# A second level of the seven-product scheme: one product of a DFT stage made jointly for two position pairs, with outputs gated from PSUM and added up in the output tensor

## The chip, the cores and the metric

The kernel runs on one core of a Trainium2 chip. The metric is device time of one execution in microseconds, as the median of several runs.

## The reference

The input is x, 2048 positions by 512 channels, all in fp32. Two branches of it are mixed by a gate per position:

```
a = x @ Re(Wh).T ;  b = x @ Im(Wh).T             # 512 x 512 DFT of the channels
y = Re(Ws) @ a - Im(Ws) @ b                      # 2048 x 2048 DFT of the positions, real part
v = (relu(x @ W_gate) * (x @ W_up)) @ W_down     # 512 -> 1792 -> 512
g = sigmoid((x * gate_w).sum(-1))
out = g * y + (1 - g) * v
```

## The kernel before

**Precision.** Each fp32 operand is split into a high part (a copy to fp32r on ScalarE, "hi") and a low part (raw minus high on VectorE, "lo"). A product is three matmuls: low x high, high x low, high x high (PARTS). A matmul has a stationary operand of 128x128 and a moving one of 128x512, and adds into one PSUM bank of 128x512.

**The seven products.** Every matrix product in the kernel is cut into 2 x 2 blocks on each side and made with seven block products instead of eight (the Strassen-Winograd form). The products are numbered 1 to 7. For each the left and right operand is a block or a sum of blocks (LEFT, RIGHT, and the sums in Left and Sequence), and the results are combined in PSUM: product 1 (X) is copied, negated, into Y's banks, products 6 and 7 add to Y, T gets a copy of Y, product 4 adds to T, product 3 adds to 5's banks M. PSUM's eight banks are four pairs: x, m, y, t.

**The stages, in order.** A warm-up of WARM matmuls of 256 columns; Direct and 13 Blocks (gate and up projections, 96 and 84 matmuls each); in between them four SpectralBlocks (channel DFT, 84 each), which write a and b to `ad` in DRAM; two Downs (the down projection, 294 each, for positions 0-1023 and 1024-2047); four Sequences (the position DFT, 336 each): for m = 0 (real) and m = 1 (imaginary) and each position pair p = 0, 1, in the order (m, p) = (0,0), (0,1), (1,1), (1,0). The last one is the subclass Last.

**A Round** is the common class of Down and Sequence. Its left operand is a Left object, which holds a high and a low part in 4-tile pieces for each product; its right operand comes in pieces jj = 0..3, for each of which a product makes 12 matmuls (two halves of 128 output channels, two tiles, three parts). The products go in the order ORDER_Z = 1, 5, 6, 3, 7, 2, 4. In a Sequence the four blocks of the DFT matrix for each jj are loaded once; the sums for products 5 and 6 are made on VectorE, those for 7 and 4 by accumulating DMAs from GpSimd's queue (`r<-r`), each so many matmuls ahead (SUM). Each product's right operand is then split by ScalarE and VectorE (HI and LO matmuls ahead).

**The outputs.** Down stores each block of v to `vd` and its negation to `zd`. Sequences of m = 0 accumulate their block of y into `zd` by DMA, which so becomes y - v. Sequences of m = 1 accumulate `zd` into their own block, load v, multiply by the gate row, add v, and store to `out`. Last does this for blocks "11" and "21" from PSUM, after loading z and v early. The gate rows (1 x 1024 positions broadcast to 128 partitions) come from `gd` in DRAM, which gate_store writes.

**The order of work.** Every operation is registered with a key: `pe(n, f)` puts matmuls at the plan's running count of matmuls, `op(key, f)` puts anything else at a given count. Plan.order then lists all instructions by a model of durations: matmuls in program order, VectorE and ScalarE by due time, at most 40 keys ahead of an operation's own key (AHEAD), SP's and GpSimd's DMAs not ahead of it. All buffers of SBUF but a few small ones are units of 4 KB per partition; there are 51 (UNITS), and an instruction that starts a new buffer waits in the list until a unit is free. Loads are issued by SP (`load`), stores and accumulations by GpSimd (`store`, `accumulate`), each queue in its listed order.

Tile names in the profile: `ch`, `cl` high and low part of a right operand, `lh`, `ll` of a left one, `r` and `hr` raw right operands, `l` and `lr` raw and summed left ones, `s` a copy of a PSUM result, `z`, `n`, `v` outputs, `gg` a gate row, `ps` PSUM. Every operation is recorded at line 125, the helper that issues it.

Of the kernel before, what the change touches and what calls it, by code (L numbers as in the profile page):

```python
# [277 lines left out]
def kernel(ctx: ExitStack, tc, xP, xG, wf, wgu, wd, cr, ci, wri, gw, out):  # L278
# [32 lines left out]
    vd, zd = (hbm(n, NT, P, KD, N) for n in ("vd", "zd"))  # L311
    wb = hbm("wb", 8, P, 4, 2, P)
    gd = hbm("gd", NT * KD, P)
    gwt = Buf(plan, "gwt", [D], kind="fixed", tile=small.tile([P, D], F32, name="gwt"))

    gs = Buf(plan, "gs", [32], kind="fixed", tile=small.tile([P, 32], F32, name="gs"))

    gx = Buf(plan, "gx", [32], kind="fixed", tile=small.tile([P, 32], F32, name="gx"))
# [267 lines left out]
    def gate(t, key):  # L586
        g = [buf("gx") for _ in range(2)]

        def read(i):
            load(g[i].all, xG[t, :, 2 * i:2 * i + 2])  # L590

        def add(i):
            x, n = g[i // 2][:, i % 2], KD * t + i
            E().vector.scalar_tensor_tensor(x, x, 1.0, gwt[:], op0=OP.mult, op1=OP.mult,
                                            accum_out=gs[:, n:n + 1])

        def sigmoid():
            ts = slice(KD * t, KD * (t + 1))
            E().scalar.activation(gs[:, ts], gs[:, ts], AF.Sigmoid)

        for i in range(2):
            op(key - 50, read, i)
        for i in range(KD):
            op(key + 10 * i, add, i)
        op(key + 50, sigmoid)

    def gate_store():
        E().vector.transpose(gx.all, gs.all)
        for i in range(0, P, 32):
            load(gd[:, i:i + 32], gx[i:i + NT * KD])  # L610

    def gate_row(p, key):

        b = buf("gg")

        def go():
            load(b.all, gd[2 * KD * p:2 * KD * (p + 1)].rearrange("(j i) p -> j (i p)", j=2).partition_broadcast(P))
        op(key, go)
        return b
# [79 lines left out]
    class Left:  # L699
# [21 lines left out]
        def split(self, m, n, key, step):  # L721
            hi, lo = self.t[m, n] = [buf(f"l{x}{m}", [4, HD], F32R) for x in "hl"]
            raw, s = self.side(m, n), slice(self.tiles[n])
            if m == 4:
                op(key, lambda: E().scalar.activation(hi[:, s], raw[:, s], AF.Copy, scale=-1.0))
                op(key + step, lambda: E().vector.scalar_tensor_tensor(
                    lo[:, s], raw[:, s], -1.0, f32(hi[:, s]), op0=OP.mult, op1=OP.subtract))
            else:
                op(key, lambda: E().scalar.copy(hi[:, s], raw[:, s]))
                op(key + step, lambda: E().vector.tensor_sub(lo[:, s], raw[:, s], f32(hi[:, s])))  # L730
# [12 lines left out]

    SUM = {5: 40, 6: 40, 7: 170, 4: 140}

    class Round:


        def __init__(self, left, counts):
# [3 lines left out]
            for x in ORDER_Z:  # L753
                for jj, n in enumerate(counts):
                    self.at[x, jj] = key
                    key += 6 * n
# [3 lines left out]
            for x in ORDER_Z:  # L760
                for jj, n in enumerate(counts):
                    pe(6 * n, self.product, x, jj)
                self.evac(x, plan.now)
# [20 lines left out]
        def evac(self, x, key):  # L784
# [6 lines left out]
            elif x == 3:  # L791
                op(key, lambda: e.vector.tensor_add(o["12"].all, M, s[6].all))
                self.done("12", key + 6)
            elif x == 7:
                op(key, lambda: e.scalar.copy(T, Y))
                op(key + 8, lambda: e.vector.tensor_add(o["22"].all, Y, s[5].all))
                self.done("22", key + 14)
            elif x == 2:
                self.middle(key)
            elif x == 4:  # L800
                self.end(key)

        def middle(self, key):
            op(key, lambda: E().scalar.copy(self.o["11"].all, PAIRS["x"].all))
            self.done("11", key + 6)

        def end(self, key):
            op(key, lambda: E().scalar.activation(self.o["21"].all, PAIRS["t"].all, AF.Copy, scale=-1.0))
            self.done("21", key + 6)


    class Down(Round):
        HI, LO = 44, 36

        def __init__(self, left, q):
            self.q = q
            super().__init__(left, (2, 2, 2, 1))

# [7 lines left out]
        def done(self, b, key):  # L826
            t, es = 2 * self.q + int(b[1]) - 1, slice(2 * int(b[0]) - 2, 2 * int(b[0]))
            o, n = self.o[b], buf("n" + b)
            op(key, lambda: store(vd[t, :, es], o.all))
            op(key + 2, lambda: E().scalar.activation(n.all, o.all, AF.Copy, scale=-1.0))  # L830
            op(key + 8, lambda: store(zd[t, :, es], n.all))


    class Sequence(Round):
        HI, LO = 31, 24

        def __init__(self, left, m, p):
            self.m, self.p = m, p
            if m:
                self.g = gate_row(p, plan.now + (20 if isinstance(self, Last) else 100))  # L840
            super().__init__(left, (2, 2, 2, 2))

        def rights(self):
            at = self.at
            for jj in range(4):
                r = {b: buf(f"r{b}") for b in BLOCKS}
                for b, key in (("11", at[1, jj]), ("12", at[5, jj]), ("22", at[6, jj] - 10), ("21", at[2, jj] - 36)):
                    op(key - 90, lambda r=r, b=b, jj=jj: load(
                        r[b].all, (cr, ci)[self.m][2 * self.p + int(b[1]) - 1, int(b[0]) - 1, jj]))
                for x, (o, i) in {5: ("11", "12"), 7: ("12", "22"), 6: ("11", "22"), 4: ("11", "21")}.items():  # L850
                    f = (lambda o, i: accumulate(o, i)) if x in (4, 7) else (lambda o, i: combine(o, o, i, 1))
                    op(at[x, jj] - SUM[x], lambda f=f, r=r, o=o, i=i: f(r[o].all, r[i].all))
                for x in ORDER_Z:
                    self.split(x, jj, r[{1: "11", 3: "22", 5: "11", 7: "12", 6: "11", 2: "21", 4: "11"}[x]])

        def place(self, b):
            return 2 * self.p + int(b[1]) - 1, slice(None), slice(2 * int(b[0]) - 2, 2 * int(b[0]))

        def gate(self, b):
            return self.g[:, int(b[1]) - 1].unsqueeze(1).to_broadcast([P, 2, N])  # L860

        def done(self, b, key):
            o = self.o[b]
            if self.m == 0:
                op(key, lambda: accumulate(zd[self.place(b)], o.all))
                return
            v = buf("v")
            op(key, lambda: accumulate(o.all, zd[self.place(b)]))
            op(key + 20, lambda: load(v.all, vd[self.place(b)]))
            op(key + 62, lambda: E().vector.tensor_mul(o.all, o.all, self.gate(b)))  # L870
            op(key + 64, lambda: E().vector.tensor_add(o.all, o.all, v.all))
            op(key + 70, lambda: load(out[self.place(b)], o.all))

    class Last(Sequence):


        def prepare(self):

            for b, k in (("11", self.base + 110), ("21", self.base + 160)):
                z, v = buf("z"), self.v[b]  # L880
                op(k - 50, lambda b=b, z=z: load(z.all, zd[self.place(b)]))
                op(k - 50, lambda b=b, v=v: load(v.all, vd[self.place(b)]))
                op(k, lambda b=b, z=z: E().vector.tensor_mul(z.all, z.all, self.gate(b)))
                op(k + 2, lambda v=v, z=z: combine(v.all, v.all, z.all, 1))

        def rights(self):
            super().rights()
            self.v = {b: buf("v") for b in ("11", "21")}
            self.prepare()

        def part(self, b, n, p, sign):
            E().vector.tensor_mul(self.o[b][:, n], p[n], self.g[:, 0])
            combine(self.v[b][:, n], self.v[b][:, n], self.o[b][:, n], sign)

        def middle(self, key):
            for n in range(2):
                op(key, self.part, "11", n, PAIRS["x"], 1)
            op(key + 8, lambda: load(out[self.place("11")], self.v["11"].all))

        def end(self, key):  # L900
            t, _, es = self.place("21")
            for n in range(2):
                op(key - 6 + 6 * n, self.part, "21", n, PAIRS["t"], -1)
                op(key - 6 + 6 * n, lambda n=n: load(out[t, :, es.start + n], self.v["21"][:, n]))
# [3 lines left out]
    WARM = 18  # L908
# [99 lines left out]
    for n in range(2):  # L1008
        for b, k in (("11", 40), ("21", 60), ("22", 70), ("12", 150)):
            op(key + k + n, la.load, b, n)  # L1010
        for m, k in ((1, 84), (5, 126), (7, 168), (6, 210), (3, 250), (2, 314), (4, 354)):
# [67 lines left out]
```

## Time and profile before

| | |
|---|---|
| median of 3 runs | 796.81 us (796.44 to 797.32) |
| the profiled execution | 796.05 us, span 794.3 us |
| TensorE busy | 787.9 us, 3474 matmuls |
| VectorE busy | 550.1 us, 610 instructions |
| ScalarE busy | 387.2 us, 419 instructions |
| GpSimd busy | 101.7 us, 146 instructions |
| HBM | 103.55 MB read, 54.53 MB written |

The span is that of one execution as the hardware profiler took it; the time of the same execution is a little longer. Engines: PE is TensorE's matmuls and PEld its weight loads, DVE VectorE, ACT ScalarE, POOL GpSimd, SP SyncE, and a q behind a name is that engine's DMA queue. Matmuls overlap one another, so that the shown duration of one is longer than the distance from one start to the next. In a line of the groups stand the operation, out<-in, the form, the count, the busy time in us and the mean in ns, and the idle time of the engine before, with what ended it. In a line of the DMA view stand the count, the size and the us from issue to landing.

### The profile page before, as it was taken

To read this page: it belongs to the slowest core of one execution; us is meant where nothing else is said; L and a number is where in the kernel's file an instruction comes from. 1 tells how busy PE (TensorE), PEld (TensorE's weight loads), DVE (VectorE), ACT (ScalarE), POOL (GpSimd) and SP (SyncE) were. 2 spreads that over 40 slices of the span, in tenths; PEclk is the share of its full clock that TensorE was granted. 3 is DMA by queue.
4 is the path that set the end of the run, shared out by engine and by line. 5 is a ranking of instruction groups with operands and counts; after the bars stand their busy time and mean duration, and the time that the engine had idled before them with its cause. 6 is when DMAs were issued, how large, how long until landed. Compare 5 with 4: busy or idle time off the path is not lost.

```text
span 794.3 us, 9282 instructions
## 1 busy us (share of the span) xinstructions
PE 787.9 (99%) x3474; PEld 652.3 (82%) x3474; DVE 550.1 (69%) x610; ACT 387.2 (49%) x419; POOL 101.7 (13%) x146
## 2 busy tenths in 40 slices
PE   9999999999999999999999999999999999999997
PEld 8888888888888888888888888888888888888885
DVE  7988755656559315978645799665746997768864
ACT  6653342424245334476556677454454566534720
POOL 1103211111112111110010012110110021101200
PEclk9999999999999999999999999999999999999999
DMA  8515534242647984387699799697989986699973
GB/s 329 240 40 209 195 139 146 93 146 93 198 146 223 350 347 168 132 281 241 222 310 356 273 317 322 159 194 209 221 225 319 246 211 183 158 313 292 310 148 132
DMA packets 50428, 175.46 MB, mean 221 GB/s; under 512 B 5840, under 2 KB 6096, under 8 KB 50384
## 3 DMA queue, kind: packets, MB, share of 16 engines
q1 hardware_dynamic: 31088, 104.62, 38.2%
q0 software_dynamic: 19296, 70.26, 31.9%
q8 instruction: 27, 0.44, 0.2%
q14 instruction: 17, 0.14, 0.1%
HBM read 103.55 MB, written 54.53 MB: 199 GB/s over the span
## 4 chain that ended last, share of the span: by engine, by line
PE 99%; DVE 0%; issue 0%
PE ps L125 99%; DVE v L125 0%; DVE z L125 0%; DVE warm L125 0%; DVE gs L125 0%
## 5 line engine op out<-in xcount | busy, mean ns | idle before, releaser
L125 PE MATMUL ps<-ch,ll 128*128 128x512 f32 x644 | 250.5, 389 | 0.0
L125 PE MATMUL ps<-cl,lh 128*128 128x512 f32 x644 | 250.5, 389 | 0.0
L125 PE MATMUL ps<-ch,lh 128*128 128x512 f32 x644 | 250.5, 389 | 0.0
L125 DVE TENSOR_TENSOR cl<-r,ch 128x1024 fp32r<-128x1024 f32 x112 | 133.8, 1221 | 40.8 <-ACT ch L125 33.0
L125 ACT CAST ch<-r 128x1024 fp32r<-128x1024 f32 x112 | 114.8, 1052 | 68.4 <-PE ps L125 26.5
L125 PEld LDWEIGHTS ps<-ch,lh 128*128 128x128 f32 x644 | 120.9, 188 | 25.2
L125 PEld LDWEIGHTS ps<-cl,lh 128*128 128x128 f32 x644 | 120.9, 188 | 25.1
L125 PEld LDWEIGHTS ps<-ch,ll 128*128 128x128 f32 x644 | 120.9, 188 | 25.0
L125 DVE TENSOR_TENSOR cl<-hr,ch 128x1024 fp32r<-128x1024 f32 (+1 forms) x56 | 59.8, 1087 | 30.1 <-ACT ch L125 27.0
L125 ACT COPY s<-ps 128x1024 f32<-128x1024 f32 x42 | 42.6, 1015 | 65.5 <-PE ps L125 61.7
L125 ACT CAST ch<-hr 128x1024 fp32r<-128x1024 f32 (+1 forms) x56 | 51.0, 941 | 9.7 <-PE ps L125 7.0
L125 ACT COPY ps<-ps 128x1024 f32<-128x1024 f32 x23 | 23.0, 998 | 67.2 <-PE ps L125 45.7
L125 ACT ACTIVATE ps<-ps 128x1024 f32<-128x1024 f32 x23 | 23.2, 1008 | 56.7 <-DVE u L125 26.1
L125 DVE TENSOR_TENSOR u<-ps,s 128x1024 f32<-128x1024 f32 x26 | 31.7, 1221 | 16.9 <-PE ps L125 13.8
L125 POOL DMA_DIRECT2D r<-r x32 | 27.8, 878 | 119.5 <-DMA r<-ci 37.4
L125 POOL DMA_DIRECT2D hd<-h x28 | 18.0, 642 | 194.8 <-DVE h L125 194.8
L125 DVE TENSOR_TENSOR r<-r,r 128x1024 f32<-128x1024 f32 x32 | 38.6, 1220 | 5.9 <-DMA r<-ci 3.4
L125 DVE TENSOR_TENSOR ll<-l,lh 128x1024 fp32r<-128x1024 f32 (+1 forms) x24 | 28.2, 1175 | 17.5 <-ACT lh L125 14.3
L125 PE MATMUL ps<-xh,wb0l 128*128 128x512 f32 x92 | 35.9, 390 | 0.0
L125 PE MATMUL ps<-xl,wb0h 128*128 128x512 f32 x92 | 35.8, 389 | 0.0
L125 PE MATMUL ps<-xh,wb1h 128*128 128x512 f32 x92 | 35.8, 389 | 0.0
L125 PE MATMUL ps<-xh,wb0h 128*128 128x512 f32 x92 | 35.8, 389 | 0.0
(199 smaller groups left out, 1227.4 us busy)
## 6 DMA issues: line engine op xcount, KB each, us to landing
hr<-hd SPq DMA_DIRECT2D x42, 512.0 KB, 5.0
r<-cr SPq DMA_DIRECT2D x32, 512.0 KB, 5.7
r<-r POOLq DMA_DIRECT2D x32, 512.0 KB, 8.6
r<-ci SPq DMA_DIRECT2D x32, 512.0 KB, 6.7
hd<-hs POOLq DMA_DIRECT2D x28, 512.0 KB, 5.5
ad<-a POOLq DMA_DIRECT2D x16, 512.0 KB, 6.1
l<-ad SPq DMA_DIRECT2D x16, 512.0 KB, 8.1
wr<-wgu SPq DMA_DIRECT2D x14, 512.0 KB, 7.2
```

Of the source, the lines that this page charges most:

```text
L125: getattr(getattr(nc, self.engine), self.name)(*map(ap, self.a), **{k: ap(x) for k, x in self.k.items()})
```

## The change

In a Sequence, product 2 (left block "12", right block "21") only goes into the output block "11" of its position pair. The change takes it out of the four Sequences. Instead, a new class Joint makes product 2 for both position pairs of one m at once: the left block is cut into two halves of the summed positions by two halves of the output channels, the right blocks of the two pairs are the two columns, each cut into the same two halves, and the 2 x 2 by 2 x 2 product is made by seven products again, each of 12 matmuls. The order of rounds is Sequence (0,0), Joint(0), Sequence (0,1), Sequence (1,1), Joint(1), Last (1,0). The sums of the Joints' right operands depend on the DFT matrices alone; `joint_sums` makes them during the Blocks and stores them in `td` in DRAM.

A Sequence's order of parts becomes 1, 5, 6, the first half of 3, 7, the second half of 3, 4; the sums for product 7 are made on VectorE (SUM from 170 to 44), the block "21" is loaded for product 4 alone, and the left operands for product 2 aren't split. The sign of T is turned, so that product 4's left operand is not negated.

The outputs: Down multiplies each block of v by 1 - g (a second sigmoid of the negated sum, a second row in `gd`) and stores it to `out`; every Sequence and Joint multiplies its block by g, from PSUM where the block is there, and accumulates it into `out` by DMA. Last loads block "21" of `out` early, adds its gated result in two halves and stores them. `vd`, `zd` and their loads and stores go. WARM goes from 18 to 15.

```diff
     hd = hbm("hd", 2, 7, P, KF // 2, N)
     ad = hbm("ad", 2, 2, 2, 2, P, 4, HD)
-    vd, zd = (hbm(n, NT, P, KD, N) for n in ("vd", "zd"))
+    od = Buf(plan, "od", (NT, P, KD, N), kind="dram", tile=out)
+    td = hbm("td", 2, 4, 2, P, 2, N)
...
+            E().scalar.activation(gs[:, 1, ts], gs[:, 0, ts], AF.Sigmoid, scale=-1.0)
+            E().scalar.activation(gs[:, 0, ts], gs[:, 0, ts], AF.Sigmoid)
...
         def late(self, key):
...
-            for i, m in enumerate(ORDER_Z):
+            for m, k in ((1, 0), (5, 48), (6, 96), (3, 144), (7, 168), (4, 240)):
                 for n in range(2):
-                    self.split(m, n, key + 48 * i - 88 + 12 * n, 8)
-
-    SUM = {5: 40, 6: 40, 7: 170, 4: 140}
+                    self.split(m, n, key + k - 88 + 12 * n, 8)
+
+    SUM = {5: 40, 6: 40, 7: 44, 4: 140}
...
+        def done(self, b, key, y):
+            o, g = self.o[b], self.g[:, int(b[1]) - 1].unsqueeze(1).to_broadcast([P, 2, N])
+            op(key, lambda: E().vector.tensor_mul(o.all, y, g))
+            op(key + 4, lambda: self.keep(od[self.place(b)], o.all))
...
     class Down(Round):
-        HI, LO = 44, 36
+        HI, LO, ONE, keep = 44, 36, 2, staticmethod(store)
...
     class Sequence(Round):
-        HI, LO = 31, 24
+        HI, LO, ONE, keep = 31, 24, 1, staticmethod(accumulate)
...
+        def parts(self):
+            return [(x, jj) for x, js in ((1, 4), (5, 4), (6, 4), (3, 2), (7, 4), (3, 4), (4, 4))
+                    for jj in (range(js) if (x, js) != (3, 4) else (2, 3))]
...
+            op(self.base + 150, lambda: load(self.v.all, od[self.place("21")]))
...
+    class Joint:
+        HI, LO = 31, 24
+        TILE = {1: "11", 3: "22", 5: 0, 6: 2, 7: 1, 2: "21", 4: 3}
+        def __init__(self, m):
+            self.m, base = m, plan.now
+            raw = [buf("jr", [4, HD]) for _ in range(2)]
+            sums = {x: buf(f"js{x}", [2, 4, P]) for x in (5, 6)}
+            half = [[buf(f"jl{x}", [2, 4, P], F32R) for x in "hl"] for _ in range(3)]
+            whole = [buf(f"jw{x}", [4, HD], F32R) for x in "hl"]
...
+            op(base - 78, lambda: combine(s[:, 0], a21, a22, -1))
+            op(base - 76, lambda: combine(s[:, 1], a21, a11, -1))
+            op(base - 74, lambda: combine(t[:, 0], a11, s[:, 0], -1))
+            op(base - 72, lambda: combine(t[:, 1], a12, t[:, 0], -1))
...
+            split(base - 60, half[0], (slice(None), 0), a11)
+            split(base - 44, half[1], slice(None), s.all)
+            split(base - 30, half[2], slice(None), t.all)
+            split(base + 20, whole, slice(None), raw[1].all)
...
+            for n, x in enumerate(ORDER_Z):
+                for hh in range(2):
+                    self.right(x, hh, base + 12 * n + 6 * hh)
+            for x in ORDER_Z:
+                for hh in range(2):
+                    pe(6, self.product, x, hh)
+                self.evac(x, plan.now)
+        def right(self, x, hh, key):
...
+            op(key - 90, read)
+            op(key - self.HI, lambda: E().scalar.copy(hi.all, raw.all))
+            op(key - self.LO, lambda: E().vector.tensor_sub(lo.all, raw.all, f32(hi.all)))
...
+        def product(self, x, hh):
+            l, c, ps = self.w[x], self.c[x, hh], self.bank(x)
+            for i in range(2):
+                for n, (a, b) in enumerate(PARTS):
+                    mm(ps, l[a][:, 2 * hh + i], c[b][:, i], ...)
...
+            elif x == 7:
+                op(key, lambda: e.scalar.activation(T, Y, AF.Copy, scale=-1.0))
+                op(key + 4, lambda: e.vector.tensor_add(o[1][:, 1], Y, s[:, 0]))
+                op(key + 10, lambda: e.vector.tensor_mul(o[1].all, o[1].all, self.gate(1).to_broadcast([P, 2, N])))
+                op(key + 14, lambda: accumulate(od[2, :, 0:2], o[1].all))
...
+    def joint_sums(m, hh, key):
+        r = {b: buf(f"jt{b}") for b in BLOCKS}
+        for n, b in enumerate(("11", "12", "22", "21")):
+            op(key + 8 * n, lambda b=b: load(r[b].all, (cr, ci)[m][2 * int(b[1]) - 2, 1, 2 * int(b[0]) - 2 + hh]))
+        for n, (o, i) in enumerate((("11", "12"), ("12", "22"), ("22", "11"), ("21", "22"))):
+            op(key + 40 + 8 * n, lambda o=o, i=i: combine(r[o].all, r[o].all, r[i].all, 1))
+            op(key + 46 + 8 * n, lambda o=o, n=n: store(td[m, n, hh], r[o].all))
...
-    WARM = 18
+    WARM = 15
...
+    for n in range(4):
+        joint_sums(n // 2, n % 2, 380 + 160 * n)
...
-    for n, (m, p) in enumerate(((0, 0), (0, 1), (1, 1), (1, 0))):
-        if n == 1:
-            start = plan.now
-            lefts[1].late(start + 336)
-        (Sequence if n < 3 else Last)(lefts[m], m, p)
+    Sequence(la, 0, 0)
+    Joint(0)
+    lefts[1].late(plan.now + 288)
+    Sequence(la, 0, 1)
+    Sequence(lefts[1], 1, 1)
+    Joint(1)
+    Last(lefts[1], 1, 0)
```

More of the change, by code (lines that the diff above doesn't have):

```diff
@@ L607, in gate_store, with gate_row @@
     def gate_store():
[L608 to L612, printed above, removed]
+        for n in range(2):
+            E().vector.transpose(gx[:, n], gs[:, n])
+            for i in range(0, P, 32):
+                load(gd[n, :, i:i + 32], gx[i:i + NT * KD, n])
+    def gate_row(n, ts, key):
         b = buf("gg")
         def go():
-            load(b.all, gd[2 * KD * p:2 * KD * (p + 1)].rearrange("(j i) p -> j (i p)", j=2).partition_broadcast(P))
+            for j, t in enumerate(ts):
+                load(b[:, j], gd[n, KD * t:KD * (t + 1)].rearrange("i p -> (i p)").partition_broadcast(P))
         op(key, go)
@@ L723, in split @@
             raw, s = self.side(m, n), slice(self.tiles[n])
[L724 to L730, printed above, removed]
+            op(key, lambda: E().scalar.copy(hi[:, s], raw[:, s]))
+            op(key + step, lambda: E().vector.tensor_sub(lo[:, s], raw[:, s], f32(hi[:, s])))
         def late(self, key):
@@ L752, in __init__ @@
             key = plan.now
[L753 to L756, printed above, removed]
+            for x, jj in self.parts():
+                self.at[x, jj] = key
+                key += 6 * counts[jj]
             self.s = {x: buf(f"s{x}") for x in (5, 6)}
@@ L759, in __init__ @@
             self.rights()
[L760 to L763, printed above, removed]
+            for x, jj in self.parts():
+                pe(6 * counts[jj], self.product, x, jj)
+                if jj == 3:
+                    self.evac(x, plan.now)
         def split(self, x, jj, raw):
@@ L792, in evac, with place @@
                 op(key, lambda: e.vector.tensor_add(o["12"].all, M, s[6].all))
[L793 removed]
+                self.done("12", key + 6, o["12"].all)
             elif x == 7:
[L795 removed]
+                op(key, lambda: e.scalar.activation(T, Y, AF.Copy, scale=-1.0))
                 op(key + 8, lambda: e.vector.tensor_add(o["22"].all, Y, s[5].all))
[L797 to L799 removed]
+                self.done("22", key + 14, o["22"].all)
             elif x == 4:
                 self.end(key)
[L803 to L805 removed]
+            if x == self.ONE:
+                self.done("11", key + 1, X)
         def end(self, key):
[L808 to L809 removed]
+            self.done("21", key, PAIRS["t"].all)
+        def done(self, b, key, y):
+            o, g = self.o[b], self.g[:, int(b[1]) - 1].unsqueeze(1).to_broadcast([P, 2, N])
+            op(key, lambda: E().vector.tensor_mul(o.all, y, g))
+            op(key + 4, lambda: self.keep(od[self.place(b)], o.all))
+        def place(self, b):
+            return 2 * self.p + int(b[1]) - 1, slice(None), slice(2 * int(b[0]) - 2, 2 * int(b[0]))
     class Down(Round):
[L813 removed]
+        HI, LO, ONE, keep = 44, 36, 2, staticmethod(store)
         def __init__(self, left, q):
[L816 removed]
+            self.q = self.p = q
+            self.g = gate_row(1, (2 * q, 2 * q + 1), plan.now + 60)
             super().__init__(left, (2, 2, 2, 1))
+        def parts(self):
+            return [(x, jj) for x in ORDER_Z for jj in range(4)]
         def rights(self):
@@ L824, in rights, with parts @@
                 self.split(x, jj, raw)
[L826 to L831, printed above, removed]
     class Sequence(Round):
-        HI, LO = 31, 24
+        HI, LO, ONE, keep = 31, 24, 1, staticmethod(accumulate)
         def __init__(self, left, m, p):
             self.m, self.p = m, p
-            if m:
-                self.g = gate_row(p, plan.now + (20 if isinstance(self, Last) else 100))
+            self.g = gate_row(0, (2 * p, 2 * p + 1), plan.now + 10)
             super().__init__(left, (2, 2, 2, 2))
+        def parts(self):
+            return [(x, jj) for x, js in ((1, 4), (5, 4), (6, 4), (3, 2), (7, 4), (3, 4), (4, 4))
+                    for jj in (range(js) if (x, js) != (3, 4) else (2, 3))]
         def rights(self):
@@ L856, in place @@
[L856 to L872, printed above, removed]
@@ L874 @@
-    class Last(Sequence):
[L877 to L884, printed above, removed]
+                for x, b in ((1, "11"), (5, "11"), (6, "11"), (3, "22"), (7, "12"), (4, "11")):
+                    self.split(x, jj, r[b])
@@ L886, in rights @@
+    class Last(Sequence):
         def rights(self):
             super().rights()
[L888 to L898, printed above, removed]
+            self.v = buf("v")
+            op(self.base + 150, lambda: load(self.v.all, od[self.place("21")]))
@@ L900, in end, with part @@
         def end(self, key):
             t, _, es = self.place("21")
+            def part(n):
+                E().vector.tensor_mul(self.o["21"][:, n], PAIRS["t"][n], self.g[:, 0])
+                combine(self.v[:, n], self.v[:, n], self.o["21"][:, n], 1)
             for n in range(2):
-                op(key - 6 + 6 * n, self.part, "21", n, PAIRS["t"], -1)
-                op(key - 6 + 6 * n, lambda n=n: load(out[t, :, es.start + n], self.v["21"][:, n]))
-    WARM = 18
+                op(key - 6 + 6 * n, part, n)
+                op(key - 6 + 6 * n, lambda n=n: load(od[t, :, es.start + n], self.v[:, n]))
@@ L1010 @@
             op(key + k + n, la.load, b, n)
[L1011 removed]
+        for m, k in ((1, 84), (5, 126), (7, 168), (6, 210), (3, 250), (4, 354)):
             if m in (3, 5, 6, 7):
```

58 lines of the change are left out of this document (49 added, 9 removed).

## The prediction

> **What bounds the kernel now.** I read the page first, its busy times and its chain of waits.
>
> ```profile
> span 794.3 us, 9282 instructions
> PE 787.9 (99%) x3474; PEld 652.3 (82%) x3474; DVE 550.1 (69%) x610; ACT 387.2 (49%) x419; POOL 101.7 (13%) x146
> PE 99%; DVE 0%; issue 0%
> 1.19 786.54 PE ps L125 x3468
> ```
>
> TensorE is the chain: one unbroken piece of matmuls from 1.19 us for 786.54 us (last line, the chain in order of time). A busy PE row says little by itself, so next I took the rate from the timeline, with both ends of the stream.
>
> ```profile
> 1.19 4.14 PE L125 MATMUL ps<-warm 128*128 128x256 f32 x18 [1.19 <-DVE gs L125]
> 5.16 1.08 PE L125 MATMUL ps<-xb11h,wf0h 128*128 128x512 f32 x4
> 788.69 0.39 PE L125 MATMUL ps<-ch,lh 128*128 128x512 f32 x1
> 789.84 0.69 DVE L125 TENSOR_TENSOR v<-v,z 128x512 f32<-128x512 f32 x1
> out<-v SPq DMA_DIRECT2D x2, 256.0 KB, 2.5
> ```
>
> The page counts 3474 matmuls; 18 are warm-up, 3456 are real, which is also what the loops give (96 + 13 x 84 + 4 x 84 + 2 x 294 + 4 x 336). Their starts run from 5.16 to 788.69: 783.53 / 3455 = 0.2268 us each, on average over the kernel, so there are no holes worth having. After the last one come two half-size products and sums on VectorE, then a 256 KB store that takes 2.5 us. Time here is the number of matmuls times 0.2268 us, plus some 12.5 us at the two ends (796.05 us in all, below), plus any holes that a change makes. The whole question is whether the other engines can feed a shorter stream.
>
> **What the change removes from TensorE.** A Sequence now runs six products instead of seven: 6 x 8 x 6 = 288 matmuls for 336, four times, so 192 go. Two Joints of 7 products x 2 halves x 6 = 84 come, so 168 return. Net 24 matmuls of the same 128x512 form: 24 x 0.2268 = **5.44 us**, all on the chain. One key of the kernel's plan is one matmul, 0.2268 us.
>
> WARM goes from 18 to 15. The 18 run from 1.19 to 5.16, 0.2206 us each for 256 columns, so three are 0.66 us. What follows must then be ready by 4.50:
>
> ```profile
> 3.85 0.69 DVE L125 TENSOR_TENSOR xb11l<-x,xb11h 128x512 fp32r<-128x512 f32 x1
> 3.99 0.79 ACT L125 CAST wf0h<-wf 128x256 fp32r<-128x256 f32 x2 [1.98 <-DMA wf<-wf]
> 4.46 0.78 DVE L125 TENSOR_TENSOR wf0l<-wf,wf0h 128x256 fp32r<-128x256 f32 x2
> ```
>
> The first two matmuls need the first half of the weight cast (done about 4.39), the next two the second half (4.78), and wf0l, done by 5.24, is wanted only after eight: there the data keep up. But 0.2206 us for 256 columns is half the later rate per column. If the slow phase ends with time, the early real matmuls run slowly and half of the 0.66 is lost; if it ends with the count of matmuls, more is lost. I take 0.5 us, with 0 and 0.66 as ends. The Trainium skill, "TensorE: Matmul & The Clock Gate", Part 1, says that the clock starts at half rate and is released after about 3.4 us of activity, a budget of time and not of matmuls, with a window that runs freely; the trace's slow phase of at most 3.97 us agrees, and by that rule the gain would be about 0.33 us.
>
> The end is unchanged in form: Last still does two half products and sums from PSUM and two half stores. Cost 0. The accumulation of the block "12" is issued some 47 keys (10.7 us) before the last matmul and has the tail besides, against the landing times below.
>
> **What it costs VectorE.** Durations first:
>
> ```profile
> L125 DVE TENSOR_TENSOR cl<-r,ch 128x1024 fp32r<-128x1024 f32 x112 | 133.8, 1221 | 40.8 <-ACT ch L125 33.0 <-PE ps L125 5.7 <-issue 1.3
> L125 ACT CAST ch<-r 128x1024 fp32r<-128x1024 f32 x112 | 114.8, 1052 | 68.4 <-PE ps L125 26.5 <-DVE r L125 21.9 <-DMA r<-cr 5.4
> 617.20 1.22 DVE L125 TENSOR_TENSOR cl<-r,ch 128x1024 fp32r<-128x1024 f32 x1
> 665.25 1.22 DVE L125 TENSOR_TENSOR ll<-l,lh 128x1024 fp32r<-128x1024 f32 x1
> 483.00:559.00 76.00, 76.00 (x337) 62.94 (x336) 51.85 (x45) 39.09 (x39) 10.38 (x13) 1.00 0.80 209
> 559.00:635.00 76.00, 76.00 (x337) 62.91 (x336) 53.59 (x47) 37.92 (x39) 10.23 (x12) 1.00 0.94 254
> 635.00:711.00 76.00, 76.00 (x337) 62.93 (x336) 62.01 (x54) 42.40 (x42) 10.22 (x12) 1.00 0.80 210
> 711.00:787.00 76.00, 76.00 (x337) 62.94 (x336) 55.37 (x50) 29.00 (x29) 9.35 (x11) 1.00 0.85 242
> sum 304.00, PE 304.00 PEld 251.73 DVE 222.82 ACT 148.42 POOL 40.17; mean PE 76.00 PEld 62.93 DVE 55.70 ACT 37.10 POOL 10.04
> ```
>
> An instruction is shown as 1.22 us, but consecutive ones overlap: from 617.20 to 665.25 VectorE ran 43 instructions without a pause, 48.05 / 42 = **1.14 us** each. The five window rows are the four Sequences (columns PE, PEld, DVE, ACT, POOL, granted clock, DMA share, GB/s): VectorE works 222.8 of 304 us, 73%.
>
> Counted in full-size instructions of 1.14 us over that stage: low parts of right operands 112 to 96 + 28 (+12); pair sums 32 to 48, because product 7's sums move from accumulating DMAs to VectorE (+16); gates and output sums 20 to 21 (+1); sums of PSUM 8 to 10 (+2); the second left operand 22 to 20 (-2); sums and low parts of the Joints' left side 0 to 12 (+12). Together +41, 46.7 us: 269 of 299 us, **90%**. On the average it fits, but not everywhere. The tightest stretch is from the preparation of the second left operand to the end of the second Joint (plan keys 576 to 1044 from the first Sequence). What has its key and its need inside is 96.5 full-size instructions: 36 for the Sequence's right operands, 14 for the Joint's, 5.9 for its left side, 2.7 for its outputs, 20 for the second left operand, 2 for the operands after it, 11 for outputs and 5 left of the Sequence before. That is 110.0 us in 468 x 0.2268 = 106.1 us: 3.9 us short if nothing runs ahead; with the plan's lead of 40 keys (9.1 us) for VectorE it has 5.2 us to spare. A second stretch is the end of the second Down:
>
> ```profile
> 460.00:480.00 20.00, 20.00 (x90) 16.55 (x89) 19.09 (x18) 16.30 (x18) 2.59 (x5) 1.00 0.92 319
> 480.00:500.00 20.00, 20.00 (x90) 16.57 (x89) 19.22 (x18) 13.43 (x14) 3.63 (x5) 1.00 1.00 310
> 415.00:483.00 68.00, 68.00 (x302) 56.31 (x301) 52.18 (x49) 44.24 (x48) 4.26 (x8) 1.00 0.90 321
> ```
>
> VectorE is at 96% from 460 on. Each Down gains four gate products (4.6 us; two low parts go from the second) where ScalarE loses four negations and two copies. Over the Down, 52.2 of 68 us is busy, so it fits; in the 20 us from 460 its 19.1 us get two of them on top, 21.4 us, 1.4 over without lead. So holes on TensorE cost between 0 and 3.9 + 1.4 = 5.3 us. I take **0.9 us**, near the low end, because the same rows show VectorE saturated for 48 us, and nearly so for 40, with TensorE whole: backlog was paid from lead. A hole would also give the lead back, so holes do not add up along one stretch.
>
> **What it costs elsewhere, hidden.** ScalarE, at 148 of 304 us, gets some 8 copies more in these stages, 8 us. The sixteen pair sums for the Joints are made during the blocks, 16 loads, 16 sums, 16 stores:
>
> ```profile
> 100.00:234.00 134.00, 134.00 (x592) 110.84 (x592) 76.55 (x109) 49.19 (x57) 18.96 (x28) 1.00 0.40 138
> ```
>
> There VectorE idles 57 us against 16 x 1.14 = 18.2 us, and DMA goes from 0.40 to at most 0.8 for 16.8 MB more. If that cover went, weights behind these loads in SP's queue would come late. The store of vd, its negated copy, the loads of v and z and the final stores go; accumulations into out come. In transfers of 512 KB the Sequence stage has 136 before and 141 after, so no relief and no new load in total. On POOL's queue 16 of the 32 r<-r accumulations go; those into out wait for the one before on the same place, 46 keys (10.4 us) or more earlier, and what queues behind them is the accumulation for product 4, asked for 140 keys ahead. Gate rows go from 2 loads to 16 smaller ones, extra sigmoids and a transpose are under 1.5 us of ScalarE and VectorE. Each 0.
>
> **Sum.** The profiled execution took 796.05 us, 0.76 below the median of 796.81. -5.44 - 0.5 + 0.9 = -5.04: 791.0 by the profiled run, **791.8** by the median.
>
> **The rivals.** *VectorE becomes the bound.* The lead isn't there, because operands come too late for it, and the full 5.3 us of holes appear: 796.81 - 5.94 + 5.3 = 796.2, no change. For: 90% average and two overfull stretches. Against: the saturated stretch of before that cost nothing.
>
> *The Joint's right operands starve (slower).* A Joint consumes a new tile every 6 matmuls, 1.36 us, each used once; a Sequence takes one per 2.72 us. All buffers are 51 units. Beside a Joint the first left operand holds 24, the Joint's left side 8, its sums, outputs and gates 4, and outputs of the Sequence before about 2: 13 remain. That units already time the loads is seen in SP's own waits, and landings are slow here:
>
> ```profile
> SPq L125 <- PE ps L125: 164.6, 47, 13.2
> r<-ci SPq DMA_DIRECT2D x11, 512.0 KB, 8.7
> z<-zd SPq DMA_DIRECT2D x2, 512.0 KB, 12.0
> DMA to landing us min/median/max: 3.2/6.9/16.8
> ```
>
> SP waited 164.6 us in the Sequences for TensorE to let go of a unit. A tile holds a raw unit for its landing + 1.05 + 1.22, a high part for 1.05 + 1.22 + 1.36, a low part for 1.22 + 1.36: landing + 8.5 unit-us. At 8.7 us of landing (from 700 to 760 us) thirteen units give one per 1.32 us: it just fits. At 12.0 one per 1.58, 0.22 x 28 tiles = 6.1 us lost; at 16.8, 16.4 us. It decides from 0.27 us a tile, landings of 12.7 us, where the saving and the measurement's 1.6 us are gone. At 15 us of landing: 0.45 x 28 = 12.5, so 790.9 + 12.5 = 803.4. Against: the Joint's loads fall where the Sequence's own pause, and some tiles are staged before it starts. The Trainium skill, "Perfetto Trace Analysis", Optimization Strategy, names consistent bubbles on the saturated engine as a sign that buffers ran out; the trace of before shows none on TensorE.
>
> *The pair sums disturb the blocks.* Each of four groups holds four units some 20 us and delays a weight load. If each delays by 2 us: 790.9 + 8 = 799.
>
> That the change doesn't drop the matmuls is not open: the loops fix 3432.
>
> **How the numbers follow.** A measurement tells 0.2%, 1.6 us, from no change. Forecast (small holes, 790.3 to 795): 0.52. VectorE as the bound, 794 to 800: 0.20, of it 0.08 faster, 0.08 same, 0.04 slower. Joint starved, 799 and up: 0.20. Blocks disturbed: 0.08, of it 0.02 same. Faster 0.60, same 0.10, slower 0.30. The low end is the full 0.66 of warm-up and no hole, 790.7, less a little for the spread of runs (0.4 below the median): 790.3. The high end, 803, reaches the middle of the starved case and leaves about one in ten above.
>
> **What would show it.** 3432 + 15 matmuls; real starts still 0.2268 us apart on average, first at about 4.6; VectorE near 269 us in the last 299, r<-r at 16. Holes on PE inside the two Joints, with SP waiting for units, would show the starving; holes with VectorE without a pause before them, the VectorE bound. The forecast is wrong if the stream has holes of over 4.3 us.

## The result: 792.72 us, and the profile after

The changed kernel takes 792.72 us (792.23 to 792.87, 4 runs), the kernel before 796.71 us: a ratio of 0.9948, 95% interval 0.993 to 0.9965. That is 4.0 us less, where 5.0 had been forecast. The profiled execution took 792.87 us, span 790.8 us.

The page's first lines after, its chain by engine, and, of the chain of waits in order of time, what ends just before its two longest pieces, these two, and the last steps between them:

```profile
span 790.8 us, 9436 instructions
PE 783.8 (99%) x3447; PEld 647.6 (82%) x3447; DVE 618.7 (78%) x680; ACT 388.6 (49%) x429; POOL 96.8 (12%) x143
PE 94%; DVE 2%; issue 1%; ACT 1%; DMA 1%; SPq 0%; DVEq 0%
31.09 1.04 ACT xh L125
32.13 0.92 ACT ps L125
33.10 519.88 PE ps L125 x2291
...
556.36 1.00 ACT jch L125
557.36 0.90 issue
558.26 0.58 ACT js L125
558.89 144.37 PE ps L125 x635
```

The matmuls are 3447 = 3432 + 15, as counted. But the chain is no longer one piece: it has other engines in it up to 33 us and inside each Joint, where a copy `js` on ScalarE ends just ahead of a matmul. Here are the stages, the first Joint in the third row and the second in the sixth (columns PE, PEld, DVE, ACT, POOL, granted clock, DMA share, GB/s):

```profile
415.00:482.00 67.00, 67.00 (x298) 55.48 (x297) 52.05 (x48) 37.41 (x41) 2.13 (x4) 1.00 0.85 298
482.00:547.00 65.00, 65.00 (x288) 53.87 (x287) 54.47 (x50) 32.06 (x33) 6.47 (x8) 1.00 0.79 231
547.00:566.00 19.00, 18.78 (x82) 14.86 (x82) 17.76 (x16) 15.44 (x19) 0.84 (x1) 1.00 1.00 334
566.00:632.00 66.00, 66.00 (x293) 54.60 (x292) 65.37 (x60) 34.03 (x35) 7.64 (x9) 1.00 0.96 297
632.00:697.00 65.00, 65.00 (x289) 53.81 (x288) 62.43 (x57) 36.70 (x38) 6.79 (x8) 1.00 0.82 222
697.00:716.00 19.00, 18.74 (x83) 15.17 (x82) 17.72 (x16) 15.53 (x19) 0.85 (x1) 1.00 1.00 332
716.00:782.00 66.00, 66.00 (x293) 54.67 (x292) 52.82 (x48) 26.21 (x27) 7.64 (x9) 1.00 0.69 181
482.00:782.00 300.00, 299.52 (x1319) 247.00 (x1318) 270.56 (x244) 159.97 (x167) 30.24 (x36) 1.00 0.84 245
```

VectorE does 270.6 us in 300; for 131 us, in the rows from 566 to 697, it is busy 127.8, and TensorE has no hole there. After 34 us the only holes are in the two Joints.

The size of a hole is read from the starts of successive matmuls, less 0.2267 us. TensorE's timeline at the first Joint's product 3, and what ScalarE does before it:

```profile
558.28 0.39 PE L125 MATMUL ps<-jch,jlh 128*128 128x512 f32 x1
558.89 0.50 PE L125 MATMUL ps<-jch,jll 128*128 128x512 f32 x1 [0.22 <-ACT js L125]
559.23 0.40 PE L125 MATMUL ps<-jcl,jlh 128*128 128x512 f32 x1
545.34 2.00 ACT L125 CAST jch<-jc 128x1024 fp32r<-128x1024 f32 x2
550.46 1.06 ACT L125 CAST jch<-jc 128x1024 fp32r<-128x1024 f32 x1 [3.12 <-issue]
551.77 1.05 ACT L125 CAST jch<-jc 128x1024 fp32r<-128x1024 f32 x1 [0.26 <-PE ps L125]
553.01 1.05 ACT L125 CAST jch<-jc 128x1024 fp32r<-128x1024 f32 x1 [0.18 <-PE ps L125]
553.96 0.58 ACT L125 ACTIVATE ps<-ps 128x512 f32<-128x512 f32 x1
554.48 3.88 ACT L125 CAST jch<-jc 128x1024 fp32r<-128x1024 f32 x4
558.26 1.05 ACT L125 COPY js<-ps 128x512 f32<-128x512 f32 x2
```

Product 3 starts 0.38 us late, and the matmul behind it is another 0.11 late. With two smaller ones the first Joint loses 0.65 us, and the second, in the same way, 0.53: **1.19 us** together. The copy of product 5's result could have run at about 555.9, when the last of product 5's matmuls ended (the 24th of the Joint, whose first starts at 550.21); it runs at 558.26, behind four casts of 3.88 us. Those are late in their turn: ScalarE stood idle for 3.12 us until 550.46. The view names nothing for that wait (`issue`); the kernel's assignment of units and the semaphores in the trace do. This cast, the fourth of the Joint, is given the unit of a high part `ch` that the Sequence's last matmuls still read. The last of them ends at 550.38, and ScalarE's wait for TensorE's semaphore ends at 550.42. In the second Joint the same wait ends with the Sequence's last matmul again, at 700.8. The first five lines show the loads of raw operands, the sixth that last matmul:

```profile
517.99 7.37 SPq L125 DMA_DIRECT2D jc<-cr  x2
528.42 7.24 SPq L125 DMA_DIRECT2D jc<-td  x4
536.81 2.83 SPq L125 DMA_DIRECT2D jc<-cr  x2
539.75 3.76 SPq L125 DMA_DIRECT2D jc<-td  x2
544.74 3.28 SPq L125 DMA_DIRECT2D jc<-cr  x2
549.99 0.39 PE L125 MATMUL ps<-ch,lh 128*128 128x512 f32 x1
```

So it is no transfer that comes late: the raw operand of this cast had been asked for at 531.37, and its landing took 3.24 us. By 544.74 eleven of the Joint's fourteen raw operands had been asked for, each in a unit of its own, and the first of these units came free after 547.52, when VectorE began the first low part. Raw operands that came early so held most of the units that the casts then lacked. No run loads them later, so whether that would close the holes is not shown.

The copy itself stands behind the four casts because it starts a unit of its own, and the plan reserves free units by program order. So two questions were open: are the holes a matter of buffers, or of engines that are full; and what did the warm-up do?

### The profile page after: what moved, and what is told of

It reads as the page before. It is cut to its first block, busy times and chain, and to the rows that moved or that the text cites. A ratio compares the mean times of both kernels' runs of the same rounds, so it can differ in the third digit from the quotient of the medians.

```text
span 790.8 us, 9436 instructions
## 1 busy us (share of the span) xinstructions
PE 783.8 (99%) x3447; PEld 647.6 (82%) x3447; DVE 618.7 (78%) x680; ACT 388.6 (49%) x429; POOL 96.8 (12%) x143
## 4 chain that ended last, share of the span: by engine, by line
PE 94%; DVE 2%; issue 1%; ACT 1%; DMA 1%; SPq 0%; DVEq 0%
PE ps L125 94%; DMA wf<-wf 1%; ACT jch L125 1%; SPq L125 0%; DVE xs L125 0%; DVE ws L125 0%; DVE xl L125 0%; DVE h L125 0%; ACT ps L125 0%; DVE v L125 0%; DVE z L125 0%; DVE wb1l L125 0%; DVE wb0l L125 0%; ACT xh L125 0%; ACT js L125 0%
## 5 line engine op out<-in xcount | busy, mean ns | idle before, releaser
L125 PE MATMUL ps<-ch,lh 128*128 128x512 f32 x580 | 225.6, 389 | 0.0
L125 PE MATMUL ps<-cl,lh 128*128 128x512 f32 x580 | 225.6, 389 | 0.0
L125 PE MATMUL ps<-ch,ll 128*128 128x512 f32 x580 | 225.6, 389 | 0.0
L125 ACT CAST ch<-r 128x1024 fp32r<-128x1024 f32 x96 | 97.5, 1052 | 73.2 <-DVE r L125 60.2
L125 PEld LDWEIGHTS ps<-ch,ll 128*128 128x128 f32 x580 | 108.9, 188 | 22.7
L125 DVE TENSOR_TENSOR cl<-r,ch 128x1024 fp32r<-128x1024 f32 x96 | 114.5, 1220 | 1.1 <-ACT ch L125 0.6
L125 ACT ACTIVATE ps<-ps 128x1024 f32<-128x1024 f32 (+1 forms) x33 | 31.6, 956 | 84.2 <-PE ps L125 38.4
L125 DVE TENSOR_TENSOR r<-r,r 128x1024 f32<-128x1024 f32 x48 | 57.1, 1218 | 0.0
L125 POOL DMA_DIRECT2D out<-z x23 | 17.1, 743 | 322.5 <-DVE z L125 322.5
L125 DVE TENSOR_TENSOR jcl<-jc,jch 128x1024 fp32r<-128x1024 f32 x28 | 32.8, 1221 | 7.0 <-ACT jch L125 6.5
```

What stands on the lines that cost most here:

```text
L125: getattr(getattr(nc, self.engine), self.name)(*map(ap, self.a), **{k: ap(x) for k, x in self.k.items()})
```

## Experiments

Each is the changed kernel with one edit, unless said otherwise.

**The warm-up.** `WARM = 18` in the changed kernel, and `WARM = 15` in the kernel before.

> The changed kernel with 18 warm-up matmuls again. Theory: with 15 the first four real matmuls ran at the slow rate (4.59 to 6.39 us) and the 136th matmul started at 33.10 us against 32.72 for the same one before, so 18 gives about 0.3 us back: 792.4 us. Rival (a time budget that ends at the same moment, data ready): the three matmuls cost 0.3 to 0.66 us: 793.0 to 793.4. Second rival: the stream is held at 33 us by VectorE and ScalarE whatever the warm-up is: 792.7.

> The kernel before with 15 warm-up matmuls and nothing else changed. Theory (the start is held by its first loads and splits until about 35 us, and real matmuls that start earlier run at the slow rate): no change, 796.7 +- 0.4. Rival (the prediction's term): -0.5, 796.2.

Measured: 792.69 us with 18 in the changed kernel (792.72 with 15); 796.60 with 15 in the kernel before (796.66 beside it; ratio 1.0001, 0.9992 to 1.001). The first theory of the first run, 0.3 us, was wrong: neither pair shows a difference, 0.03 and 0.06 us, though the interval would still allow 0.6. The profiled starts show why. With 15 the first real matmul starts at 4.52 to 5.21 us (twelve profiles, those of the runs below among them), with 18 at 5.16 and 5.19; but the 400th real matmul starts anywhere between 95.41 and 96.73 with 15, and at 95.75 (before) and 96.22 with 18. With 15, one or both of two things eat the lead: waits for casts of the first loads, and the slow rate, which by the trace's record of the granted clock lasted to some moment between 4.4 and 7.3 us. In the changed kernel's profile:

```profile
1.20 3.57 PE L125 MATMUL ps<-warm 128*128 128x256 f32 x15 [1.20 <-DVE warm L125]
4.59 1.96 PE L125 MATMUL ps<-xb11h,wf0h 128*128 128x512 f32 x4
```

Four matmuls in 1.96 us here, against 1.08 in the kernel before. After that the stream meets a second place, where VectorE is nearly the bound (third column of busy times, in the kernel before):

```profile
20.00:40.00 20.00, 20.00 (x90) 16.35 (x89) 18.85 (x25) 12.24 (x15) 2.13 (x4) 1.00 0.58 236
```

The 121st real matmul needs a copy in PSUM (`ps`) on ScalarE, which stands behind two casts (`xh`), the first of which waits for a sum of VectorE (`xs`). With 15 warm-up matmuls in the kernel before, that matmul waits 0.46 us and starts at 32.52; in the changed kernel it waits 0.39 and starts at 33.10, after the two ScalarE lines of the chain above. Of the twelve profiles with 15, five have such a wait of 0.3 us or more there; most of the others had lost the lead to the slow rate before, and one (the run `e3_order` below) passed without a wait and kept 0.35 us of lead on the kernel before.

**The Joint taken back.** Product 2 in the Sequences, no Joints, no sums for them; all the rest of the change stays.

```
-    Joint(0)
-    Joint(1)
...
     def parts(self):
+        return [(x, jj) for x in ORDER_Z for jj in range(4)]     # and x = 2 split again, ONE = 2
```

> The changed kernel with product 2 back in the four Sequences and no Joints and no sums for them; outputs, gates, product 7's sums on VectorE and 15 warm-up matmuls as in the changed kernel. Theory: 24 matmuls more (5.44 us) and the Joints' holes gone (-1.1 us): 792.7 + 4.3 = 797.0 us, about the kernel before, so that the whole gain is the Joints'. Rival: the new outputs and sums gain or lose by themselves; then it lies over 1 us from 797.0, and VectorE shows holes on TensorE at the end of the second Down or in the Sequences.

Measured: 796.70 us, ratio to the kernel before 1.0004 (0.9995 to 1.0012), with no hole after 34 us. The theory held: the whole gain is the Joints'; the outputs added up in `out`, the gates and product 7's sums on VectorE, taken together, neither gain nor lose.

**The copy in ScalarE's order.**

```
+            kept = buf("js5")                 # sums[5] and later the copies of products 5 and 6
...
-            self.c, self.s = {}, buf("js")
+            self.c, self.s = {}, kept
```

> The changed kernel, but the Joint's copies of products 5 and 6 go to the unit that its left sums had, so that they need no new unit. Theory: in the order of the changed kernel the copy of product 5 stands behind four casts of right operands on ScalarE, because it starts a new unit and units are reserved by program order; product 3 then waits about 0.6 us in each Joint. With the copy in its place both holes go: -1.0 us, 791.7 us. Rival (ScalarE itself has too much to do there, 9.1 of 10 us, or operands come too late): the hole moves to a product behind it and the time stays at 792.7.

Measured: 792.15 us (0.9945, 0.9933 to 0.9958). The copy now stands between casts, and product 3 doesn't wait; but the second half of product 6 waits for its low part, 0.47 us in each Joint, 0.94 together where 1.19 had been. So it was half the theory and half the rival: the hole moved ahead to an operand.

> The changed kernel, but the Joint's products in the order 1, 5, 6, 2, 7, 3, 4, so that product 3 comes 36 matmuls after product 5's copy is possible rather than 12. Theory (the copy of product 5 is what product 3 waits for): the hole at product 3 goes, and unless product 7 waits in its place for the copy of product 6, -1.0 us: 791.7. Rival (operands or ScalarE too slow): no change, 792.7.

The edit is `ORDER` (1, 5, 6, 2, 7, 3, 4) for `ORDER_Z` in Joint. The output work of the second pair moves from product 7 to product 3, and the split of the left operand of products 2 and 4 comes 16 matmuls earlier. Measured: 793.45 us (0.9971, 0.9959 to 0.9983), 0.7 us above the changed kernel, with intervals that just overlap; by the starts of matmuls its Joints lose 2.3 us instead of 1.19. Product 3's hole went, and product 2, which has its place now, waits for its low parts, 0.78 us and 0.11 behind it for the second half alone, in each Joint. So the dependency on the copy was not the only cause but the first of several things that were late together. The earlier split is work for ScalarE and VectorE in the same stretch, and its share was not separated.

**Buffers.** `UNITS = 49`, and `UNITS = 50`.

> The changed kernel with 49 units of SBUF instead of 51, everything else by the same rules. Theory (buffers are what makes the Joints wait): the holes inside the two Joints, together 1.2 us in the changed kernel, grow to over 3 us, and the time to 795 us or more, with holes nowhere else in the Sequences. Rival (ScalarE or VectorE is too slow there, or the copy's place alone): the Joints' holes stay near 1.2 us, 792.7 +- 0.5.

> The changed kernel with 50 units. With 49 the holes outside the start were 9.5 us against 1.7 with 51. Theory (buffers are at the edge): between the two, 794 to 798 us, with the holes in the Joints again. Rival (49 fell over a threshold of its own, such as a lost buffer in the SpectralBlocks): as with 51, 792.7.

Measured: 800.95 us with 49 (ratio to before 1.0058, 1.0046 to 1.0071) and 794.69 us with 50 (0.9978, 0.9969 to 0.9987), against 792.72 with 51. The waits of TensorE, and the two Joints' windows, with 49:

```profile
PE ps L125 <- ACT js L125: 4.2, 2, 2.1
PE ps L125 <- DVE jcl L125: 1.8, 2, 0.9
PE ps L125 <- DVE vl L125: 1.5, 1, 1.5
547.00:570.00 23.00, 19.98 (x87) 15.75 (x86) 18.82 (x17) 17.72 (x21) 0.84 (x1) 1.00 0.95 320
705.00:725.00 20.00, 17.01 (x74) 13.28 (x73) 19.31 (x17) 17.02 (x20) 0.84 (x1) 1.00 1.02 347
```

With 49 the Joints lose 7.2 us, for the copy as with 51 and for low parts, and a SpectralBlock loses 1.95 (`vl`), which I hadn't expected. With 50 the Joints lose 2.5 us and a SpectralBlock 1.7. Every engine has as many instructions as with 51. Two units less turn the gain into a loss: the theory of buffers holds, with one more place than it named. (The number of units also sets the order in which the plan lists its instructions, so that waiting for units and standing in another order are not told apart.)

The other way round, four units are left to the Joint for longer, by later loads of the next Sequence's first blocks:

```
-  ("11", at[1, jj])
+  ("11", at[1, jj] + (0 if self.m == self.p else 28))     # and 36 in the last run
```

> The changed kernel, but the Sequences that follow a Joint load their four blocks 11 28 matmuls later, so that four units stay with the Joint's operands for 6 us longer. Theory (buffers): the copies and casts come in time and both Joints' holes go, -1.0 us: 791.7 us. Rival (VectorE and ScalarE at over 9 of 10 us in the Joint are the bound): no change, 792.7. Third way: the first product of the next Sequence waits for its block: holes at the start of those Sequences, 793 or more.

> Both the later blocks 11 and the Joint's copies in the old unit. Theory: the same as with the later blocks alone, 791.6 us; if the copy's place in ScalarE's order is a cause of its own, this one is lower than that by 0.3 to 0.6 us.

> The blocks 11 after a Joint 36 matmuls later instead of 28. With 28 the Joints kept 0.95 us of holes' worth of 1.2: at product 2, behind its low part. Theory (buffers): a further 0.3 to 0.6 us, 791.7; if VectorE's work in the Joint is what is left, no change against 792.14; if the blocks now come late, holes at the start of the next Sequence and 793 or more.

Measured: 792.14, 792.33 and 792.06 us (ratios 0.9946, 0.9948 and 0.9943, the last 0.9931 to 0.9956). The copies' holes go, in the run with 36 as in that with 28. In the one with 36, ScalarE's timeline has the copy of product 5 back in its place, and of TensorE's waits one short one for a low part is left in the Joints:

```profile
553.88 2.94 ACT L125 CAST jch<-jc 128x1024 fp32r<-128x1024 f32 x3
556.72 0.58 ACT L125 COPY js<-ps 128x512 f32<-128x512 f32 x1
557.19 1.06 ACT L125 CAST jch<-jc 128x1024 fp32r<-128x1024 f32 x1
PE ps L125 <- DVE jcl L125: 0.2, 1, 0.2
```

By the starts of matmuls the Joints still lose 0.98 us with 36 and 0.94 with 28, now at product 2, behind its low part. ScalarE's idle 3.12 us at the start of the Joint is still there, since its cast waits again for the Sequence's last matmul. The medians are 0.4 to 0.7 us below the changed kernel's, the intervals overlap: more units at this place help a little or not at all, and none of these kernels can be called faster than the changed one. Both edits together gave nothing beyond either: with the copy in the old unit, the hole of 0.47 us at product 6's second half is in each Joint as it was without the later loads.

**VectorE.** One run takes 16 sums from it, one adds 16.

```
-    SUM = {5: 40, 6: 40, 7: 44, 4: 140}
+    SUM = {5: 40, 6: 40, 7: 142, 4: 140}     # 7 by accumulating DMA
+    SUM = {5: 40, 6: 40, 7: 44, 4: 44}       # 4 on VectorE too
```

> The changed kernel with the sums for product 7 made by accumulating DMAs again, asked for 142 matmuls ahead: 16 sums (18 us) less for VectorE in the Sequences. If VectorE bounds the stage, the time falls by 0.5 us or more. Theory (it doesn't: 130 us without a pause and without a hole): no gain; units are held longer by the slower sums, so 792.7 to 796.

> The changed kernel with the sums for product 4 on VectorE as well (44 matmuls ahead instead of an accumulating DMA 140 ahead): 16 sums, 18 us more, of them 8 or so in the stretch of 106 us that the prediction found tightest. By its sum, 104.5 full-size instructions x 1.14 = 119.1 us against 115.2 us with the plan's lead: VectorE becomes the bound and TensorE gets some 4 us of holes there, 796 us or more. If VectorE still has room, 792 to 793.

Measured: 795.25 us with 16 fewer (0.9983, 0.9974 to 0.9992), 797.94 us with 16 more (1.0016, 1.0007 to 1.0025). The stage with fewer, then the second Sequence, the second Joint and the last Sequence with more:

```profile
482.00:782.00 300.00, 297.64 (x1310) 245.14 (x1309) 252.84 (x228) 159.49 (x167) 44.02 (x52) 1.00 0.94 272
632.00:697.00 65.00, 63.61 (x279) 51.99 (x278) 64.78 (x58) 33.28 (x34) 1.70 (x2) 1.00 0.59 182
697.00:716.00 19.00, 16.76 (x70) 12.47 (x69) 19.00 (x20) 14.77 (x17) 2.54 (x3) 1.00 0.93 279
716.00:782.00 66.00, 65.85 (x290) 54.13 (x290) 62.42 (x57) 31.69 (x33) 3.39 (x4) 1.00 0.56 161
```

With 17.7 us less for VectorE the kernel is 2.5 us slower, and the first Joint's hole at product 3 is still there, 0.42 us and 0.11 behind it: VectorE's work as a whole did not bound it. Two holes come in the Sequence of the second left operand (658 and 661 us, 1.9 us), and a larger one in the second Joint. With 16 more, VectorE is busy for 19.00 of 19 us in the Joint, and TensorE has 5.7 us of holes between 658 and 721 us where it had 0.5. The prediction's sum, taken on in the expectation above, gives 3.9 for that load. So VectorE's edge seems to lie between the 270.6 us of the changed kernel and some 18 us more. But 1.9 us of the holes are at the same two matmuls as with 16 fewer. They come neither of the amount of VectorE's work nor of accumulating DMAs into `r`, of which the run with 16 more has none. In both runs VectorE goes without a pause from 648 to 663 us in another order than in the changed kernel: product 6's first low part, which the first hole waits for, stands behind work on the second left operand and an output, at 656.75 and 657.23 us, where the changed kernel makes it at 652.40. Why the plan lists it so late in both was not separated. The run with 16 more also keeps the raw blocks "21" in their units until 44 matmuls ahead instead of 140, so that buffers may have a part in the rest of its loss.

## Why the prediction was right, and where it was not

- **24 matmuls, 5.44 us: right.** 3432 real matmuls ran; from the 400th real one to the last, the profiled runs took 692.93 us before and 688.81 after, 4.12 less = 5.44 - 1.19 of Joint holes - 0.13. Without the Joints the time is that of before.
- **The warm-up, 0.5 us: wrong.** No gain is seen (796.60 against 796.66). The step that failed is "there the data keep up", checked at the first eight matmuls alone: what counts is the stretch to 33 us, where VectorE works nearly without pause, and there the lead that the slow rate has left is given back in most profiles. The row of before that would have told it is that of VectorE from 20 to 40 us, 18.85 us busy of 20.
- **Holes of 0.9 us: near in size, 1.19 us, wrong in place and cause.** They were set down to VectorE's two tightest stretches. There are none there, so that the size fits by luck. The sum for the first of them also has a slip: the second Joint ends at key 1032, not 1044, and by the same count the stretch is 6.6 us short without lead instead of 3.9, and has 2.5 us to spare with it. VectorE's work was well forecast (269 us in 299; 270.6 in 300 measured), and so was the lead's worth: saturation for 131 us cost nothing, and one more load of 18 us cost 5, of which 1.9 are at a place where the run with 16 fewer loses the same.
- **ScalarE, "each 0": wrong.** Its busy time fits, at 160 of 300 us, and it still ends the Joint's longest hole: a copy out of PSUM has 12 matmuls' time, 2.7 us, in a Joint, and ScalarE gets 9.1 us of work in the 10 us around it because the casts come in a bunch, each as a unit comes free. The wait of a PSUM copy wasn't priced.
- **The rival of the starved Joint: its mechanism is there, at a small price.** It counted the units that raw operands, high and low parts hold, and took the landings for what lengthens that; landings of a Joint's operands were 3.2 to 8.6 us, far from the 12.7 us from which it would have decided, and raw operands came early and not late. What ran short was units for the casts. Tiles staged before the Joint, which the prediction counted against this rival, are, by the count of loads above, what held them. That the units only just sufficed is shown by 50 and 49: 2.0 and 8.2 us more, with 1.3 and 6.0 us more of holes in the Joints.
- **The rival of VectorE and that of disturbed blocks** didn't come about: the stretch of the blocks has no hole after 34 us, and no change of pace (the 400th to the 1000th real matmul take 136.12 us before and 136.07 after).

Of the 0.9 us between the forecast median, 791.8, and the measured 792.72, 0.5 is the warm-up and 0.3 the holes; 0.1 is within the spread of the runs.

## What to carry to other kernels

In a kernel that TensorE fills, fewer matmuls are worth their full time only as long as the new part's operands have buffers: count what is alive there, unit by unit, and try one unit less to see how near the edge is. An engine that is half idle on average can still end a hole when a shortage of buffers bunches its work, so price each short wait (a copy out of PSUM between two products) with the queue that stands before it. A gain at the start counts only when nothing later in the first stage is already the bound.

## What the runs showed of the hardware

Each hole on TensorE was followed by a second, small one: the matmul behind the one that waited starts 0.34 us after it instead of 0.23 (558.89 and 559.23 above), some 0.11 us more, after every hole of 0.2 us or more that the profiles have behind the slow start. A short wait costs that on top.

The slow rate at the start ended at different times: with 15 warm-up matmuls the trace has the full clock granted from 4.4 to 4.8 us on in four profiles, 5.2 to 6.6 in five, and 7.0 to 7.3 in three, though the warm-ups began at 1.19 or 1.20 us in all. The stretch at the full clock lasted 781.65, 785.07, 788.48 or 791.89 us, values that lie 3.41 us apart. The Trainium skill, "TensorE: Matmul & The Clock Gate", Part 1, says that the window runs freely, so that the moment varies from run to run; these runs agree, by more than the 0.5 us either way that it gives. With 18 the two profiles had the full rate from the first real matmul, at 5.16 and 5.19 us; the full clock was granted from 5.10 and 5.16 on.
